# Cosines from squared half-angle sines in a filter generator, with its products and six tiles' statistics in other places

## The chip, the cores and the metric

The kernel runs on one core of one Trainium2 chip. The metric is the device time of one execution in microseconds (us), as the median of the runs shown; less is better. A core has engines that each work through an instruction queue of their own, in order: PE (TensorE, matmuls), DVE (VectorE), ACT (ScalarE), POOL (GpSimd) and SP, which here only issues DMAs. They wait for each other by semaphores.

## The reference, cut to what matters

Four layers on a 2048 x 640 activation: a long convolution (A), an attention (B), and both again with the same weights. Every layer is added to its input and starts with a layer norm.

```
def _A_ref(u, A_re, A_im, B_re, B_im, C_re, C_im, log_dt, Dskip):
    dt = jnp.exp(log_dt)[:, None]
    A, Bc, Cc = A_re + 1j * A_im, B_re + 1j * B_im, C_re + 1j * C_im
    P = jnp.exp((dt * A)[:, :, None] * l[None, None, :])      # l = 0 .. 2047
    K = jnp.einsum("dn,dnl,dn->dl", Cc, P, dt * Bc).real      # 640 channels, 128 states
    ...                                                       # y = u convolved with K
    return y + u * Dskip[None, None, :]
x = x + _A_ref(_layernorm(x), ...)
x = x + _B_ref(_layernorm(x), ...)
x = x + _A_ref(_layernorm(x), ...)
x = x + _B_ref(_layernorm(x), ...)
```

The change lies in the making of K, the filter of both convolutions: for every channel, state and time a complex exponential, that is a real exponential times a cosine and a sine, summed over the 128 states.

## The kernel before, in words

The program first makes the filter (`_kgen`), then its five spectra together with the first convolution (`kernel_spectra` and what follows), then attention, convolution and attention. In the profile `_kgen` ends at about 281 us of 2950.

**Generation.** Time is split as l = 32 i + s, so that an exponential of l is a product of one of i (64 values, tables with a 1) and one of s (32 values, tables with a 2). The states lie on the 128 partitions. The 640 channels go through in 20 units of 32, u = 0 to 19; each tile below is 128 x 1024 fp32, or near it. For each unit:

- PE makes phases into PSUM (`phase_first`, L424, tile `ph`, one buffer) in two halves h = 0 and 1, and exponents (`sizes`, L467, tile `pe`, two buffers) in three pieces k = 0, 1, 2, from bf16 tables `ta`, `tb`, `tm`.
- DVE turns a phase into an integer (`turns`, L433, tile `z`, one buffer) and shifts its whole turns out (`fraction`, L438, tile `f`, four buffers).
- ACT takes from each `f` the absolute value (L456, tile `fa`, one buffer), the sine (L457) and, from `fa` with a tile `halfpi` as bias, the cosine (L459). That is `trig`, twice a unit. From each `pe` it takes an exponential (`exps`, L475 and L477). Sines and exponentials are in different function tables, and an ACT_TABLE_LOAD stands at each change. To halve these, two units make a pair: exponentials of an even and the following odd unit stand together, and sines of the odd and the next even one.
- DVE multiplies exponentials with cosines and sines in six products (`products`, L485 to L494).
- PE sums over the states (`sums`, L504, tile `pk`), ACT copies the sums (`store`, L513), and after four units SP writes them to DRAM (`kd`). POOL clears the first columns of two tables a unit (L448, L449).

These steps are staggered by hand: in pass u of the loop ACT works on unit u, DVE on the phases of u + 1 and on the products of u - 1, PE on the sums of u - 2. `manual_schedule` keeps PE, ACT and DVE in the order in which the code is written. SP's and POOL's queues are ordered by a scheduler.

**What lies around it.** Ahead of the loop, `kg_tables` makes the tables on DVE and ACT and sends them through DRAM by DMA (SP queue). The first phase needs `tb`, the first exponent `tm` (L280). The activation x is loaded by eight DMAs of 640 KB (`load_x`, L685); tiles 0 to 3 of its 16 need the first two of these, tiles 4 to 7 the next two. Layer-norm statistics of a tile (`stats`: two L693, one L695) are DVE work: tiles 0 to 5 after the products of the last unit (u = 20), 6 to 9 in pass 21, and 10 to 15 among the butterflies of the first spectrum. Once PE has read the last table, `conv_weights` loads 4 MB of transform weights `wf` (L614). POOL loads the first channels of the filter back as `Rk` (L799), and PE starts the first spectrum (`raw`, L637, tile `zk`; ACT evicts it as `Ak`, L639; DVE adds and subtracts, L650 and on).

Of the kernel before, what the change touches and what calls it, by code (L numbers as in the profile page):

```python
# [202 lines left out]
class Net:  # L203
# [8 lines left out]
    def setup(self, ctx):  # L212
# [4 lines left out]
        self.halfpi = self.cp.tile([P, 1], F32, name="halfpi")  # L217
        nc.vector.memset(self.halfpi, 0.5 * math.pi)
# [144 lines left out]
    def _kgen(self, ctx):  # L363
# [39 lines left out]
        C1, S1, C2, S2, M1, M2, E1R, F, FA, Z, PH, PE_, PK, KST = ({} for _ in range(14))  # L403
# [23 lines left out]
        def turns(u, h):  # L427

            if (u, h) not in PH:
                phase_first(u, h)  # L430
            pp = PH.pop((u, h))
            Z[u, h] = bp.tile([P, 1024], I32, tag="z", bufs=1, name=f"z{u}{h}")
            nc.vector.tensor_scalar(Z[u, h], pp, 2.0**23, None, ALU.mult)  # L433

        def fraction(u, h):

            f = bp.tile([P, 1024], I32, tag="f", bufs=4, name=f"f{u}{h}")
            nc.vector.tensor_scalar(f, Z.pop((u, h)), 9, 9, ALU.logical_shift_left, ALU.arith_shift_right)  # L438
            F[u, h] = f

        def phase(u, h):
            turns(u, h)
            fraction(u, h)

        def trig(u, h):
            if h == 0:
                C1[u], S1[u] = big("c1", u, 33), big("s1", u, 33)
                nc.gpsimd.memset(C1[u][:, :, :, 0:1], 1.0)  # L448
                nc.gpsimd.memset(S1[u][:, :, :, 0:1], 0.0)  # L449
                s, c = swap(S1[u])[:, :, :, 1:33], swap(C1[u])[:, :, :, 1:33]  # L450
            else:
                C2[u], S2[u] = big("c2", u, 32, 3), big("s2", u, 32, 3)
                s, c = swap(S2[u]), swap(C2[u])
            f = F.pop((u, h))
            fa = bp.tile([P, 1024], F32, tag="fa", bufs=1, name=f"fa{u}{h}")
            nc.scalar.activation(fa, f, AF.Abs)  # L456
            nc.scalar.activation(s, f.rearrange("p (a d s) -> p a d s", a=2, d=16), AF.Sin,  # L457
                                 scale=TWO_PI / 2.0**23)
            nc.scalar.activation(c, fa.rearrange("p (a d s) -> p a d s", a=2, d=16), AF.Sin,  # L459
                                 scale=-TWO_PI / 2.0**23, bias=self.halfpi)  # L460
# [18 lines left out]
        def products(u, k):  # L479

            tt = nc.vector.tensor_tensor
            if k == 0:
                E1R[u] = big("e1r", u, 64, 2)
                er, m1, c1 = (fl(a[u]) for a in (E1R, M1, C1))
                tt(er[:, :, 32:64], m1[:, :, 32:64], c1[:, :, 0:32], ALU.mult)  # L485
                tt(er[:, :, 0:32], m1[:, :, 0:32], c1[:, :, 32:0:-1], ALU.mult)
            elif k == 1:
                m1, s1 = (fl(a.pop(u)) for a in (dict(M1), S1))
                nc.vector.scalar_tensor_tensor(m1[:, :, 32:64], m1[:, :, 32:64], -1.0, s1[:, :, 0:32],
                                               op0=ALU.mult, op1=ALU.mult)  # L490
                tt(m1[:, :, 0:32], m1[:, :, 0:32], s1[:, :, 32:0:-1], ALU.mult)
            else:
                tt(C2[u], C2[u], M2[u], ALU.mult)
                tt(S2[u], S2[u], M2[u], ALU.mult)  # L494
# [12 lines left out]
        def store(u):  # L507
# [5 lines left out]
            nc.scalar.activation(kst[:, :, 8 * g : 8 * g + 8], PK[u].rearrange("p (d i) -> p i d", d=8), AF.Copy)  # L513
# [15 lines left out]
        with tc.manual_schedule(engines=engines):  # L529
            for h in range(2):  # L530
                phase(0, h)
            for u in range(n + 3):
                now, nxt, prod, tot = u < n, u + 1 < n, 0 < u <= n, 2 <= u < n + 2
                odd = u % 2 == 1
                if u >= 3:
                    store(u - 3)
                if now and not odd:
                    trig(u, 0)
                if prod:
                    products(u - 1, 0)  # L540
                if now:
                    sizes(u, 0)
                    if odd:
                        exps(u, 0)
                if nxt:
                    phase_first(u + 1, 0)
                if now:
                    sizes(u, 1)
                    if odd:
                        exps(u, 1)  # L550
                if tot:
                    sums(u - 2, range(0, 1) if odd else range(0, 4))
# [1102 lines left out]
```

## Time and profile before

| What | us |
|---|---|
| median of 3 runs (2950.36 to 2952.25) | 2951.08 |
| the profiled execution: its time | 2951.75 |
| the profiled execution: its span, first to last instruction | 2950.0 |
| ahead of the loop (to the last `fraction` of unit 0) | 0 to 47.7 |
| first pair's exponentials | 54.4 to 62.8 |
| generation in a steady rhythm (the loads of the exponential table, 8 pairs) | 76.55 to 257.85 |
| first matmul of a spectrum | 280.75 |

The profiled execution is 0.67 us over the median, and 1.75 us of its time lie outside the span. In a row of the profile, "x16" counts instructions, then come their busy time in us and the mean of one in ns, then the idle time of that engine just ahead of them with what ended it. In the timeline the columns are start, duration, engine, line, operation and tiles; a bracket holds the idle time ahead. An instruction may start before the one ahead of it on its engine has ended, so that the distance of two starts, its pitch, is what a row of instructions costs. L numbers are lines of the kernel before, unless "after" is said.

### The profile page before, as it was taken

How to read it: one execution, taken by the hardware profiler on the slowest of the kernel's cores; microseconds unless marked ns; L12 is line 12 of the kernel's file. 1: busy time of each engine (PE TensorE's matmuls, PEld its weight loads, DVE VectorE, ACT ScalarE, POOL GpSimd, SP SyncE). 2: the span in 40 equal slices, each digit the busy share in tenths (PEclk: the TensorE clock that was granted, in tenths of full speed). 3: DMA queues.
4: the chain of work that ended last, by engine and by line, in shares of the span. 5: the costliest groups of instructions: out<-in, count | busy, mean ns of one | idle time of the engine just before them, and what ended most of it. 6: DMA issues, size and time to landing. Idle time of an engine off the chain costs nothing. (4 is left out here: it accounts for less than half of the span.)

```text
span 2950.0 us, 71583 instructions
## 1 busy us (share of the span) xinstructions
PE 2683.3 (91%) x29916; PEld 1557.6 (53%) x29916; DVE 2353.5 (80%) x2820; ACT 2386.6 (81%) x2905; POOL 294.5 (10%) x514
## 2 busy tenths in 40 slices
PE   2566989898899999999999998998999999999999
PEld 0234978774344444444444687773444444444444
DVE  7999999934688888888888699726788888888885
ACT  5997333455899999999999634338999999999997
POOL 0000011100210101011110011001101111111101
PEclk9767999998999999999999999998999999999999
DMA  6124545532211111111111256231111111111211
GB/s 147 35 30 141 193 114 112 147 116 84 93 33 37 32 37 34 35 34 35 36 34 33 93 115 160 67 126 47 36 34 39 51 32 36 51 35 34 55 31 31
DMA packets 156101, 196.31 MB, mean 67 GB/s; under 512 B 66220, under 2 KB 123532, under 8 KB 152148
## 3 DMA queue, kind: packets, MB, share of 16 engines
q1 hardware_dynamic: 119704, 141.90, 16.3%
q0 software_dynamic: 33776, 48.08, 7.9%
q8 instruction: 239, 3.92, 0.6%
q10 hardware_dynamic: 2288, 1.64, 0.2%
q14 instruction: 94, 0.77, 0.1%
HBM read 111.47 MB, written 48.55 MB: 54 GB/s over the span
## 5 line engine op out<-in xcount | busy, mean ns | idle before, releaser
L1360 ACT ACTIVATE ring<-ring 128x1024 f32<-128x1024 f32 (+1 forms) x680 | 738.2, 1086 | 0.4 <-DVE ring L1351 0.3
L1335 ACT ACTIVATE pt<-scb 128x1024 f32<-128x1024 f32 x684 | 692.1, 1111 | 26.5 <-PE scb L1325 24.8
L1335 ACT ACTIVATE pt<-scd 128x1024 f32<-128x1024 f32 x684 | 699.6, 1135 | 14.5 <-PE scd L1325 12.7
L1351 DVE COPY ring<-scd 128x1024 f32<-128x1024 f32 x307 | 375.2, 1222 | 82.4 <-PE scd L1325 63.0
L1351 DVE COPY ring<-scb 128x1024 f32<-128x1024 f32 x307 | 374.7, 1220 | 80.0 <-PE scb L1325 63.1
L1325 PE MATMUL scb<-qpb,kt 62*128 62x512 f32 x2048 | 365.5, 445 | 29.5 <-DVE ring L1351 14.4
L1325 PE MATMUL scd<-qpd,kt 62*128 62x512 f32 x2048 | 364.2, 444 | 19.1 <-ACT pt L1335 6.7
L1391 PE MATMUL pob<-pt,vt 128*32 128x256 f32 x5472 | 368.0, 387 | 0.0
L1391 PE MATMUL pod<-pt,vt 128*32 128x256 f32 x5472 | 367.1, 386 | 0.0
L1325 PEld LDWEIGHTS scb<-qpb,kt 62*128 62x128 f32 x2048 | 169.7, 186 | 249.2 <-ACT pt L1335 135.6
L1325 PEld LDWEIGHTS scd<-qpd,kt 62*128 62x128 f32 x2048 | 169.2, 185 | 239.8 <-ACT pt L1335 144.7
L1377 DVE SCALAR_TENSOR_TENSOR zh<-zh,zm 128x1024 f32<-128x1024 f32 x198 | 239.6, 1210 | 0.0
L1391 PEld LDWEIGHTS pob<-pt,vt 128*32 128x32 f32 x5472 | 143.3, 109 | 168.2 <-issue 109.4
L1391 PEld LDWEIGHTS pod<-pt,vt 128*32 128x32 f32 x5472 | 143.3, 109 | 165.6 <-issue 106.8
L1391 PE MATMUL pob<-ring,vt 128*32 128x256 f32 x2456 | 164.8, 381 | 0.4 <-ACT ring L1360 0.4
L1391 PE MATMUL pod<-ring,vt 128*32 128x256 f32 x2456 | 163.9, 379 | 0.4 <-ACT ring L1360 0.4
L1423 POOL DMA_DIRECT2D dn<-on x62 | 43.7, 705 | 1189.0 <-DVE on L1422 1152.1
L1429 POOL DMA_DIRECT2D rc<-ivd x248 | 126.5, 516 | 112.4 <-DMA ivd<-dn 108.4
L1460 DVE TENSOR_TENSOR x<-pyd,x 128x320 f32<-128x320 f32 x147 | 71.7, 488 | 77.2 <-PE pyd L1473 77.2
L1460 DVE TENSOR_TENSOR x<-pyb,x 128x320 f32<-128x320 f32 x147 | 71.7, 488 | 75.9 <-PE pyb L1473 75.8
L1473 PE MATMUL pyb<-wo,ot 128*32 128x320 f32 x1176 | 106.7, 434 | 6.3 <-DVE on L1422 5.6
L1473 PE MATMUL pyd<-wo,ot 128*32 128x320 f32 x1176 | 106.7, 434 | 5.7 <-DVE on L1422 4.9
(391 smaller groups left out, 4081.3 us busy)
## 6 DMA issues: line engine op xcount, KB each, us to landing
Akh<-kh SPq DMA_DIRECT2D x10, 2048.0 KB
rc<-ivd POOLq DMA_DIRECT2D x248, 64.0 KB, 2.2
kh<-Ak SPq DMA_DIRECT2D x5, 2048.0 KB
qhd<-qh SPq DMA_DIRECT2D x40, 256.0 KB
qld<-ql SPq DMA_DIRECT2D x40, 256.0 KB
qpb<-qhd SPq DMA_DIRECT2D x256, 40.0 KB
qpd<-qhd SPq DMA_DIRECT2D x256, 40.0 KB
ot<-on SPq DMA_DIRECT2D x216, 40.0 KB
```

The costliest lines, as they stand in the source:

```text
L1325: nc.tensor.matmul(sc[:, 512 * par : 512 * par + 512], kt[rows, 128 * t : 128 * t + 128], qps[nb, hg][rows, f].rearrange("p a c -> p (a c) ...
L1335: nc.scalar.activation(pt, sc, AF.Exp, scale=SCALE)
L1351: nc.vector.tensor_copy(cols, sc)
L1360: nc.scalar.activation(cols, cols, AF.Exp, scale=SCALE)
L1377: nc.vector.scalar_tensor_tensor(h, a, c[k], f, op0=ALU.add, op1=ALU.mult)
L1391: nc.tensor.matmul(po[32 * j : 32 * j + 32, 256 * f : 256 * f + 256], v[:, t], pt[j], start=(t == 0), stop=(t == 15))
L1423: nc.gpsimd.dma_start(den, on[20:128:32].rearrange("j (c r) -> j c r", c=32))
L1429: nc.gpsimd.dma_start(inv[32 * j : 32 * j + 32], self.ivd[hg % 2, j : j + 1].to_broadcast([32, 512]))
L1460: nc.vector.tensor_tensor(xh, py, xh, ALU.add)
L1473: nc.tensor.matmul(py[j : j + m], o[:, 128 * i + j : 128 * i + j + m], w[:, c0 : c0 + n], start=start, stop=stop)
```

## The change: what it does

Lines L430 to L620 of the kernel after hold it.

- **Cosines.** cos t = 1 - 2 sin(t/2)^2. `trig` now takes from `f` the sine of half the angle into the place of the cosine (after: L446) and the sine (L447). A new ACT instruction squares the first in place (`squares`, L454). The absolute value, the tiles `fa` and `halfpi` and the old cosine are gone. ACT has as many instructions as before.
- **Where the squares stand.** In odd passes each stands behind its two sines. In even passes they are put off (list `left`) and stand between the exponentials of that unit (`fill`).
- **Products.** The missing factor and the half are put into the products: five of six are now `scalar_tensor_tensor` with two constants, (c - 0.5) * m or (+-0.25 s) * m; `store` copies with a scale of 4.
- **Products behind phases.** `turns` writes `f` directly and `fraction` works in place (tile `z` is gone). Between a `turns` and its `fraction` there now stands a product.
- **Statistics.** Those of tiles 0 to 5 move from pass 20 to pass 0, ahead of the `turns` of unit 1; `load_x` stands earlier in the code, but SP's queue has its DMAs at the same places as before, and PE's instructions stand in the same order too.

On ACT, an even unit (4) and what follows it, before (c and s are cosine and sine tables, m exponentials; the number behind a name is the unit or a buffer):

```order
L475 ACT_TABLE_LOAD
L475 ACTIVATE m_4_732<-pe_637 128x16x64
L475 ACTIVATE m_4_732<-pe_643 128x16x64
L477 ACTIVATE m_4_733<-pe_735 128x2x16x32
L513 ACTIVATE kst_279<-pk_646 128x64x8
L475 ACTIVATE m_5_747<-pe_744 128x16x64
L475 ACTIVATE m_5_747<-pe_753 128x16x64
L477 ACTIVATE m_5_748<-pe_770 128x2x16x32
L456 ACTIVATE fa_780<-f_681 128x1024
L457 ACT_TABLE_LOAD
L457 ACTIVATE s_5_777<-f_681 128x2x16x32
```

The same place after:

```order
L469 ACT_TABLE_LOAD
L469 ACTIVATE m_4_730<-pe_639 128x16x64
L454 ACTIVATE c_4_630<-c_4_630 128x2x16x32
L469 ACTIVATE m_4_730<-pe_645 128x16x64
L454 ACTIVATE c_4_686<-c_4_686 128x2x16x32
L471 ACTIVATE m_4_731<-pe_734 128x2x16x32
L513 ACTIVATE kst_277<-pk_648 128x64x8
L469 ACTIVATE m_5_747<-pe_744 128x16x64
L469 ACTIVATE m_5_747<-pe_753 128x16x64
L471 ACTIVATE m_5_748<-pe_768 128x2x16x32
L446 ACT_TABLE_LOAD
L446 ACTIVATE c_5_775<-f_681 128x2x16x32
```

Two squares (L454) have come between the three exponentials of unit 4, and the absolute value ahead of the second table load has gone.

On DVE, the products of unit 5 with the phases of unit 7, before:

```order
L485 TENSOR_TENSOR e1r_872<-m_5_747,c_5_776 128x32x32
L486 TENSOR_TENSOR e1r_872<-m_5_747,c_5_776 128x32x32
L433 TENSOR_SCALAR z_917<-ph_878 128x1024
L438 TENSOR_SCALAR f_919<-z_917 128x1024
L489 SCALAR_TENSOR_TENSOR m_5_747<-m_5_747,s_5_777 128x32x32
L491 TENSOR_TENSOR m_5_747<-m_5_747,s_5_777 128x32x32
L433 TENSOR_SCALAR z_956<-ph_953 128x1024
L438 TENSOR_SCALAR f_958<-z_956 128x1024
L493 TENSOR_TENSOR c_5_849<-c_5_849,m_5_748 128x1024
L494 TENSOR_TENSOR s_5_850<-s_5_850,m_5_748 128x1024
```

And after:

```order
L490 SCALAR_TENSOR_TENSOR e1r_866<-c_5_775,m_5_747 128x32x32 x2
L431 TENSOR_SCALAR f_911<-ph_872 128x1024
L492 SCALAR_TENSOR_TENSOR m_5_747<-s_5_776,m_5_747 128x32x32
L436 TENSOR_SCALAR f_911<-f_911 128x1024
L492 SCALAR_TENSOR_TENSOR m_5_747<-s_5_776,m_5_747 128x32x32
L431 TENSOR_SCALAR f_947<-ph_944 128x1024
L490 SCALAR_TENSOR_TENSOR c_5_846<-c_5_846,m_5_748 128x1024
L436 TENSOR_SCALAR f_947<-f_947 128x1024
L494 TENSOR_TENSOR s_5_847<-s_5_847,m_5_748 128x1024
```

Each `fraction` (after: L436) has moved one product behind its `turns` (L431).

On DVE in the opening, after, with the semaphores that each instruction waits for:

```order
L436 TENSOR_SCALAR f_289<-f_289 128x1024 [waits DVE_49]
L723 BN_STATS st_316<-x 128x6 [waits DMAHW1_49,DMAHW0_49]
L723 BN_STATS st_316<-x 128x6
L725 BN_AGGR mv_65<-st_316 128x2 [waits DVE_49]
L723 BN_STATS st_320<-x 128x6 x2
L725 BN_AGGR mv_65<-st_320 128x2 [waits DVE_49]
L723 BN_STATS st_324<-x 128x6 x2
L725 BN_AGGR mv_65<-st_324 128x2 [waits DVE_49]
L723 BN_STATS st_328<-x 128x6 x2
L725 BN_AGGR mv_66<-st_328 128x2 [waits DVE_49]
L723 BN_STATS st_332<-x 128x6 [waits DMAHW3_49,DMAHW2_49]
```

Between the last `fraction` of unit 0 and the first `turns` of unit 1, which stood next to each other, there are now six tiles' statistics (the fifth begins in the last row, and the `turns` follows the sixth); the first waits for two DMA queues, the fifth tile (st_332) for two others.

The diff's core:

```diff
         def turns(u, h):
...
-            Z[u, h] = bp.tile([P, 1024], I32, tag="z", bufs=1, name=f"z{u}{h}")
-            nc.vector.tensor_scalar(Z[u, h], pp, 2.0**23, None, ALU.mult)
+            f = F[u, h] = bp.tile([P, 1024], I32, tag="f", bufs=4, name=f"f{u}{h}")
+            nc.vector.tensor_scalar(f, pp, 2.0**23, None, ALU.mult)
         def fraction(u, h):
-            f = bp.tile([P, 1024], I32, tag="f", bufs=4, name=f"f{u}{h}")
-            nc.vector.tensor_scalar(f, Z.pop((u, h)), 9, 9, ALU.logical_shift_left, ALU.arith_shift_right)
-            F[u, h] = f
+            f = F[u, h]
+            nc.vector.tensor_scalar(f, f, 9, 9, ALU.logical_shift_left, ALU.arith_shift_right)
         def trig(u, h):
...
-            fa = bp.tile([P, 1024], F32, tag="fa", bufs=1, name=f"fa{u}{h}")
-            nc.scalar.activation(fa, f, AF.Abs)
-            nc.scalar.activation(s, f.rearrange("p (a d s) -> p a d s", a=2, d=16), AF.Sin,
+            nc.scalar.activation(halves(u, h), f, AF.Sin, scale=0.5 * TWO_PI / 2.0**23)
+            nc.scalar.activation(swap(S2[u]) if h else swap(S1[u])[:, :, :, 1:33], f, AF.Sin,
                                  scale=TWO_PI / 2.0**23)
-            nc.scalar.activation(c, fa.rearrange("p (a d s) -> p a d s", a=2, d=16), AF.Sin,
-                                 scale=-TWO_PI / 2.0**23, bias=self.halfpi)
+        def halves(u, h):
+            return swap(C2[u]) if h else swap(C1[u])[:, :, :, 1:33]
+        def squares(u, h):
+            nc.scalar.activation(halves(u, h), halves(u, h), AF.Square)
...
+                if k == 0 or (k, part) == (2, 0):
+                    nc.vector.scalar_tensor_tensor(out, a, 0.5, b, op0=ALU.subtract, op1=ALU.mult)
+                elif k == 1:
+                    nc.vector.scalar_tensor_tensor(out, a, (-0.25, 0.25)[part], b, op0=ALU.mult, op1=ALU.mult)
+                else:
+                    nc.vector.tensor_tensor(out, a, b, ALU.mult)
...
+            left = []
+            def fill():
+                if left:
+                    squares(*left.pop(0))
             for u in range(n + 3):
...
                 if now and not odd:
                     trig(u, 0)
+                    left.append((u, 0))
...
+                if u == 0:
+                    for t in range(6):
+                        self.stats(t)
                 if nxt:
-                    phase(u + 1, 0)
+                    turns(u + 1, 0)
...
                 if prod:
-                    products(u - 1, 1)
-                if now:
-                    trig(u, 0 if odd else 1)
+                    products(u - 1, 1, (0,))
+                if nxt:
+                    fraction(u + 1, 0)
+                if prod:
+                    products(u - 1, 1, (1,))
+                if now and odd:
+                    trig(u, 0)
+                    squares(u, 0)
+                elif now:
+                    trig(u, 1)
+                    left.append((u, 1))
...
-                    else:
-                        exps(u, 0)
-                        sizes(u, 2)
-                        exps(u, 1)
-                        exps(u, 2)
...
-                for t in {n: range(6), n + 1: range(6, 10)}.get(u, ()):
-                    self.stats(t)
+                elif now:
+                    exps(u, 0)
+                    fill()
+                    sizes(u, 2)
+                    exps(u, 1)
+                    fill()
+                    exps(u, 2)
+                if u == n + 1:
+                    for t in range(6, 10):
+                        self.stats(t)
```

More of the change, by code (lines that the diff above doesn't have):

```diff
@@ L402, in _kgen @@
         units += [(2, r, 512 + 16 * r, 64, 64) for r in range(4)]
-        C1, S1, C2, S2, M1, M2, E1R, F, FA, Z, PH, PE_, PK, KST = ({} for _ in range(14))
+        C1, S1, C2, S2, M1, M2, E1R, F, PH, PE_, PK, KST = ({} for _ in range(12))
         KST[0, 0] = bp.tile([P, 64, 32], F32, tag="kst", bufs=2, name="kst00")
@@ L512, in store @@
             kst = KST[q, h]
-            nc.scalar.activation(kst[:, :, 8 * g : 8 * g + 8], PK[u].rearrange("p (d i) -> p i d", d=8), AF.Copy)
+            nc.scalar.activation(kst[:, :, 8 * g : 8 * g + 8], PK[u].rearrange("p (d i) -> p i d", d=8), AF.Copy,
+                                 scale=4.0)
             if g == 3:
@@ L530, in _kgen @@
             for h in range(2):
-                phase(0, h)
+                turns(0, h)
+                fraction(0, h)
+            left = []
+            def fill():
+                if left:
+                    squares(*left.pop(0))
             for u in range(n + 3):
@@ L534, in _kgen @@
                 odd = u % 2 == 1
+                if u == 0:
+                    self.load_x()
+                    nc.sync.dma_start(self.ident, ins["c_id"])
                 if u >= 3:
@@ L564, in _kgen @@
                 if nxt:
-                    phase(u + 1, 1)
+                    turns(u + 1, 1)
                 if prod:
-                    products(u - 1, 2)
+                    products(u - 1, 2, (0,))
+                if nxt:
+                    fraction(u + 1, 1)
+                if prod:
+                    products(u - 1, 2, (1,))
                 if tot:
                     sums(u - 2, range(5, 8) if odd else range(7, 8))
-                if now:
-                    if odd:
-                        trig(u, 1)
-                    else:
-                        exps(u, 0)
-                        sizes(u, 2)
-                        exps(u, 1)
-                        exps(u, 2)
-                if u == 0:
-                    self.load_x()
-                    nc.sync.dma_start(self.ident, ins["c_id"])
-                for t in {n: range(6), n + 1: range(6, 10)}.get(u, ()):
-                    self.stats(t)
+                if now and odd:
+                    trig(u, 1)
+                    squares(u, 1)
+                elif now:
+                    exps(u, 0)
+                    fill()
+                    sizes(u, 2)
+                    exps(u, 1)
+                    fill()
+                    exps(u, 2)
+                if u == n + 1:
+                    for t in range(6, 10):
+                        self.stats(t)
                 if u == n:
```

42 lines of the change are left out of this document (19 added, 23 removed).

## The prediction

> **What bounds the kernel now.** I looked first at the page of the profile, then at the busy times by stretch, since the change touches only the generation of the filter, which ends near 281 us. Columns of the second view: stretch, its length, then busy time (and instructions) of PE, weight loads, DVE, ACT, POOL, then granted clock and DMA.
>
> ```profile
> span 2950.0 us, 71583 instructions
> ...
> 76.55:257.85 181.30, 110.85 (x2208) 58.51 (x2208) 169.85 (x162) 172.72 (x176) 7.12 (x34) 0.69 0.18 29
> 280.75:297.10 16.35, 15.82 (x144) 15.74 (x141) 15.80 (x44) 4.69 (x5) 0.00 (x0) 1.00 0.84 221
> ```
>
> The first stretch is eight pairs of units, 181.30 / 8 = 22.66 us each. ACT is busy in 172.72 us of it, DVE in 169.85. Two engines so near to full need the timeline of a pair. This is ACT's, from one load of the exponential table to the next:
>
> ```profile
> 76.55 1.28 ACT L475 ACT_TABLE_LOAD   x1
> 77.84 1.94 ACT L475 ACTIVATE m<-pe 128x1024 f32<-128x1024 f32 x2
> 79.96 1.02 ACT L477 ACTIVATE m<-pe 128x1024 f32<-128x1024 f32 x1 [0.18 <-PE pe L467]
> 80.88 0.59 ACT L513 ACTIVATE kst<-pk 128x512 f32<-128x512 f32 x1
> 81.36 1.03 ACT L475 ACTIVATE m<-pe 128x1024 f32<-128x1024 f32 x1
> 82.63 1.02 ACT L475 ACTIVATE m<-pe 128x1024 f32<-128x1024 f32 x1 [0.24 <-PE pe L467]
> 84.18 1.02 ACT L477 ACTIVATE m<-pe 128x1024 f32<-128x1024 f32 x1 [0.53 <-PE pe L467]
> 85.10 1.05 ACT L456 ACTIVATE fa<-f 128x1024 f32<-128x1024 int32 x1
> 86.17 1.28 ACT L457 ACT_TABLE_LOAD   x1
> ...
> 88.44 1.15 ACT L459 ACTIVATE c<-fa,halfpi 128x1024 f32<-128x1024 f32 x1
> 89.62 1.06 ACT L456 ACTIVATE fa<-f 128x1024 f32<-128x1024 int32 x1
> 90.59 1.04 ACT L457 ACTIVATE s<-f 128x1024 f32<-128x1024 int32 x1
> 91.53 1.14 ACT L459 ACTIVATE c<-fa,halfpi 128x1024 f32<-128x1024 f32 x1
> 92.58 0.57 ACT L513 ACTIVATE kst<-pk 128x512 f32<-128x512 f32 x1
> ...
> 99.21 1.28 ACT L475 ACT_TABLE_LOAD   x1
> ```
>
> ACT never waits for DVE here. It waits three times for PE, 0.18 + 0.24 + 0.53 = 0.95 us. Each wait also loses the overlap of two instructions, 0.10, since neighbours start 0.92 apart (79.96 to 80.88) though one lasts 1.02. So 1.26 us of the 22.66 are lost to waits, and 21.40 are work. DVE does wait for ACT:
>
> ```profile
> L485 DVE TENSOR_TENSOR e1r<-m,c 128x1024 f32<-128x1024 f32 x16 | 19.5, 1221 | 6.5 <-issue 6.5
> L489 DVE SCALAR_TENSOR_TENSOR m<-m,s 128x1024 f32<-128x1024 f32 x16 | 19.5, 1218 | 0.0
> ...
> 82.65 1.22 DVE L433 TENSOR_SCALAR z<-ph 128x1024 int32<-128x1024 f32 x1
> 83.90 0.69 DVE L438 TENSOR_SCALAR f<-z 128x1024 int32<-128x1024 int32 x1
> 84.51 1.22 DVE L489 SCALAR_TENSOR_TENSOR m<-m,s 128x1024 f32<-128x1024 f32 x1
> 85.65 1.22 DVE L491 TENSOR_TENSOR m<-m,s 128x1024 f32<-128x1024 f32 x1
> ```
>
> The 6.5 us idle ahead of the first product (x16, one a unit) have no releaser in the view; the product reads exponentials and cosines, so I put them down to ACT. A unit on DVE is six products at a pitch of 1.14 (84.51 to 85.65), two turns at 1.25 and two fractions at 0.61: 6.84 + 3.72 = 10.56, a pair 21.1. So ACT sets the pace at 22.66, DVE has 1.5 us to spare.
>
> **ACT in a pair.** Out go four absolute values, three at 0.97 (89.62 to 90.59) and one at 1.07 ahead of the table load, and four cosines. A cosine costs 1.05 ahead of a copy (91.53 to 92.58) and 1.18 ahead of an absolute value (88.44 to 89.62), which rewrites the `fa` that the cosine reads. Two are of this kind, one stands ahead of a copy, and one ahead of a load, where it lasts its 1.14. That is 3.98 + 4.55 = 8.53. In come four sines of half angles and four squares. A half sine is the old sine with another constant, 0.94 to 0.97. No row shows a square of this size: it is bounded by the exponential's 0.92 below and the cosine's 1.18 above. I take 0.95, for like the absolute value and the sine it has no bias tile, and the tile it reads was written two instructions earlier, which cost the old cosine nothing (its `fa` too was two earlier). Eight at 0.95 are 7.60; the last exponential and the last sine now stand ahead of table loads and lose their overlap, 0.22. In: 7.82. **Work saved: 0.7 a pair.**
>
> The Trainium skill ("ScalarE: Activation LUTs", What ACT_TABLE_LOAD costs) says that an ACTIVATE takes the same time for every function, that a pointer operand adds about 93 ns, and that neighbours overlap by about 93 ns; an estimate from it for the square is 186 + 0.833 x 1024 - 93 = 946 ns. By it the sum below stays; by the cosine's row it would lose 8.3 us.
>
> Then the waits. PE refills two `pe` buffers behind ACT. With squares between the even unit's exponentials, the third piece is ready when ACT comes (0.28 gone), and so is the odd unit's second (0.34 gone): PE has the time of two squares more. The last wait is a path through PE:
>
> ```profile
> 81.54 1.06 PE L467 MATMUL pe<-kg,tm 48*128 48x512 bf16 x2
> ```
>
> From this start to the odd unit's last exponential (84.18) go 2.64 us. After the change this matmul can start when the even unit's third exponential has freed its buffer: 1.29 (load) + 0.92 + 0.95 + 0.92 + 0.95 + 1.02 = 6.05 into the pair. So the last exponential starts at 8.7; ACT would come at 1.29 + 3 x 0.92 + 2 x 0.95 + 0.48 + 2 x 0.92 = 8.27. It waits 0.4 instead of 0.63. **Waits saved: 0.8 a pair** (none at worst, 1.26 at best). Pair: 22.66 - 0.7 - 0.8 = 21.15; eight pairs 12.1.
>
> **DVE in a pair.** The products have the same size; `scalar_tensor_tensor` costs what `tensor_tensor` does (1218 and 1221). With a product between, a fraction no longer waits for its turns: 1.25 becomes 1.14, a unit 8 x 1.14 + 2 x 0.61 = 10.34, a pair 20.7. That is under ACT's 21.15, so it earns nothing by itself but keeps DVE from becoming the bound. The first product of an even unit needs the second exponential, which one square pushes back by 0.95; the hidden side of that is DVE's slack, 22.66 - 21.1 before, and now 21.15 - 20.7 = 0.45. DVE then runs a little later behind ACT, and ACT does not wait for it: the fraction that starts at 83.90 is the one that ACT takes up behind the copy of 92.58, 8 us on. POOL's clearing of columns follows the products of the unit two before.
>
> Against the interleaving speaks the Trainium skill ("VectorE: DVE Perf Modes", The DRAIN you can't avoid): the next operation starts only when the pipe is empty, and a semaphore between chained operations costs nothing more. By that rule a pair stays at 21.1 on DVE, still just under 21.15, and no saved wait beyond the forecast's would count. The pitch of 1.25 behind a dependent turns against 1.14 between products does not agree with it here.
>
> **Opening and tail.** Between the first pair's exponentials and the load at 76.55 stand four absolute values and four cosines (8.5); then there will be four half sines and two squares (5.9 with lost overlaps), for the other two squares come behind the load: **2.6 saved.** At the end these two have to be paid:
>
> ```profile
> 270.44 1.23 DVE L485 TENSOR_TENSOR e1r<-m,c 128x1024 f32<-128x1024 f32 x1 [2.37 <-ACT c L459]
> ```
>
> DVE's last six products wait for the last unit's cosine. On the way there from the last exponential load: two squares more (1.9), waits less (0.3), the last exponential's overlap (0.1), and half sine and square against absolute value and cosine (2.0 against 2.2): **1.5 lost.**
>
> **The statistics.** Where they go DVE waits for PE, and PE for a table's DMA; what they need was issued long before, and what they cost stands at their old place, where the seventh tile starts 6.01 us after the first:
>
> ```profile
> 4.04 2.72 SPq L685 DMA_DIRECT2D x<-in_A_u  x4
> 20.00 0.36 SPq L277 DMA_DIRECT2D hdth<-hth  x1
> 25.24 1.29 SPq L280 DMA_DIRECT2D tb<-hdth  x3
> 47.07 0.69 DVE L438 TENSOR_SCALAR f<-z 128x1024 int32<-128x1024 int32 x1
> 53.14 1.01 PE L467 MATMUL pe<-kg,tm 48*128 48x512 bf16 x2 [7.37 <-DMA tm<-hdare]
> 55.04 1.23 DVE L433 TENSOR_SCALAR z<-ph 128x1024 int32<-128x1024 f32 x1 [7.28 <-PE ph L424]
> 277.26 0.88 DVE L693 BATCH_NORM_STATS2 st<-x 128x6 f32<-128x320 f32 x2
> 283.27 0.83 DVE L693 BATCH_NORM_STATS2 st<-x 128x6 f32<-128x320 f32 x2
> ```
>
> They run from 47.76 to 53.8, the turns behind them is due at 55.04: hidden, with 1.3 to spare. The `tb` DMAs of 25.24 read what a DMA issued at 20.00, behind the four x loads on the same queue, had written, so I take x to have landed by then. At the old place they free nothing:
>
> ```profile
> 296.05 1.02 ACT L639 ACTIVATE Ak<-zk 128x1024 f32<-128x1024 f32 x1 [2.55 <-PE zk L637]
> 297.19 0.64 DVE L650 TENSOR_TENSOR B<-Ak 128x512 f32<-128x512 f32 x1
> ```
>
> DVE's last piece starts 0.12 after PE and ACT have delivered it (297.07), and PE is full from 280.75 on (15.82 of 16.35). **0 to 0.1.**
>
> **Sum.** 12.1 + 2.6 - 1.5 = 13.2 us by which the first spectrum starts earlier; all behind it keeps its order and moves along. The profiled execution's 2951.75 becomes 2938.6. It is 0.67 over the median, so on the median: 2951.08 - 13.2 = 2937.9.
>
> **Rivals.**
>
> *A wait for x (slower).* If the six tiles had to wait for all eight x loads, of which the last is issued at 78.37,
>
> ```profile
> 78.37 0.59 SPq L685 DMA_DIRECT2D x<-in_A_u  x1
> ```
>
> DVE would stand until 79 at least, statistics to 85, and the next turns 30 us late: 2951 + 30 - 13 = 2968. From a landing at 47.8 + 1.3 + 13.2 = 62.3 on the change loses. For it: x is one tile. Against it: the first and the fifth tile wait for two queues each, as separate loads would have it. Chance 0.05.
>
> *DVE becomes the bound.* A phase already comes late to DVE in some pairs:
>
> ```profile
> 109.67 1.22 DVE L433 TENSOR_SCALAR z<-ph 128x1024 int32<-128x1024 f32 x1 [0.66 <-PE ph L424]
> ```
>
> PE makes it behind the exponents, which now wait for ACT longer: if the wait grows to 1.0 in every pair and DVE cannot use it up as lag, a pair is 20.7 + 1.0 = 21.7 and the sum 7.7 + 1.1 = 8.8: 2942.3. For it: only 0.45 of slack. Against: the wait shrinks as DVE falls behind. Chance 0.15.
>
> *A square as dear as a cosine.* 36 squares at 0.23 more take 8.3 away: 4.9 are left, 2946.2; with all waits kept too, 2953. Chance 0.06.
>
> *The gain doesn't arrive.* The first spectrum needs `Rk` and weights by DMA:
>
> ```profile
> Rk<-kd POOLq DMA_DIRECT2D x1, 1024.0 KB, 8.6
> 264.66 0.69 POOL L799 DMA_DIRECT2D Rk<-kd  x1
> ```
>
> It landed at 273.3, 7.5 ahead of use, and its issue follows the same stores and moves with them. If something here stood still the time stays 2951. Chance 0.04.
>
> **How the numbers follow.** The forecast has the remaining 0.70. Its ends: no wait left gives 0.7 + 1.26 a pair, 15.7 + 2.6 - 1.1 = 17.2, 2933.9; all waits kept gives 0.7 a pair, 5.6 + 2.6 - 1.8 = 6.4, 2944.7. The range, 2934 to 2945, holds these and the second rival. A change of 0.2%, 5.9 us, is about what a measurement of this kernel can tell from none. Faster by more: forecast and second rival, 0.85. Within: third rival and the fourth, 0.10. Slower: 0.05, the first.
>
> **What would show it.** Loads of the exponential table 21.15 apart on ACT, the first near 74, the tenth near 243; a square at 1.04, no table load beside it; one wait of 0.3 to 0.4 for `pe` in a pair; fractions 1.14 behind what stands ahead; the first statistics at 47.8 with no wait for x; the first product of unit 19 near 257 and the first spectrum's matmul near 267.5. The prediction is wrong if ACT waits for DVE in the pairs, or if the spectrum starts early and the end does not move by as much.

## The result, and the profile after it

The changed kernel took 2934.24 us (median of 4 runs, 2931.56 to 2935.08) against 2950.72 for the kernel before on the same chip (2949.54 to 2952.25): a ratio of 0.9942, interval 0.9925 to 0.9960. It is 16.5 us faster; 13.2 were forecast. Four repetitions and near copies of it below (e1, e3, e10, e11) came out 18.8 to 20.2 us faster. The profiled execution took 2934.5. L numbers of the changed kernel are its own.

The page's first line, and the busy times by stretch of the same two stretches as before (length, then PE, weight loads, DVE, ACT, POOL, granted clock, DMA):

```profile
span 2932.7 us, 71549 instructions
...
74.40:244.01 169.61, 114.13 (x2220) 59.56 (x2210) 166.41 (x163) 166.47 (x176) 6.78 (x34) 0.70 0.16 31
268.48:284.83 16.35, 15.96 (x141) 15.87 (x142) 10.75 (x27) 4.69 (x5) 0.00 (x0) 1.00 0.77 221
```

Eight pairs now take 169.61 us, 21.20 a pair, where they took 22.66. The first spectrum starts at 268.48, 12.27 sooner than at 280.75, but the span is 17.3 shorter: some 5 us come from behind the generation. First one pair on ACT, in the timeline, with the load that ends it (the sines between are left out):

```profile
74.40 1.28 ACT L469 ACT_TABLE_LOAD   x1
75.70 1.02 ACT L469 ACTIVATE m<-pe 128x1024 f32<-128x1024 f32 x1
76.62 1.07 ACT L454 ACTIVATE c<-c 128x1024 f32<-128x1024 f32 x1
77.59 1.01 ACT L469 ACTIVATE m<-pe 128x1024 f32<-128x1024 f32 x1
78.49 1.06 ACT L454 ACTIVATE c<-c 128x1024 f32<-128x1024 f32 x1
79.44 1.02 ACT L471 ACTIVATE m<-pe 128x1024 f32<-128x1024 f32 x1
80.34 0.61 ACT L513 ACTIVATE kst<-pk 128x512 f32<-128x512 f32 x1
80.82 1.96 ACT L469 ACTIVATE m<-pe 128x1024 f32<-128x1024 f32 x2
83.11 1.03 ACT L471 ACTIVATE m<-pe 128x1024 f32<-128x1024 f32 x1 [0.33 <-PE pe L461]
84.15 1.28 ACT L446 ACT_TABLE_LOAD   x1
...
95.60 1.28 ACT L469 ACT_TABLE_LOAD   x1
```

A square stands between exponentials without a table load, at a pitch of 0.97 and 0.95 (76.62 to 77.59, 78.49 to 79.44). Two of the three waits for `pe` are gone, the third is 0.33. Now DVE, in the opening, in a pair, and at the last unit:

```profile
47.94 0.69 DVE L436 TENSOR_SCALAR f<-f 128x1024 int32<-128x1024 int32 x1
48.55 0.88 DVE L723 BATCH_NORM_STATS2 st<-x 128x6 f32<-128x320 f32 x2
...
54.43 0.21 DVE L725 BATCH_NORM_AGGREGATE mv<-st 128x2 f32<-128x12 f32 x1
55.56 1.23 DVE L431 TENSOR_SCALAR f<-ph 128x1024 int32<-128x1024 f32 x1 [0.92 <-PE ph L422]
...
82.58 1.23 DVE L431 TENSOR_SCALAR f<-ph 128x1024 int32<-128x1024 f32 x1
83.71 1.22 DVE L492 SCALAR_TENSOR_TENSOR m<-s,m 128x1024 f32<-128x1024 f32 x1
84.84 0.70 DVE L436 TENSOR_SCALAR f<-f 128x1024 int32<-128x1024 int32 x1
85.45 1.23 DVE L492 SCALAR_TENSOR_TENSOR m<-s,m 128x1024 f32<-128x1024 f32 x1
...
258.14 2.36 DVE L490 SCALAR_TENSOR_TENSOR e1r<-c,m 128x1024 f32<-128x1024 f32 x2 [2.64 <-ACT c L454]
```

The six tiles' statistics start right behind the fraction, wait for nothing, and leave 0.92 us of waiting for PE (0.42 in the repetition e1). Turns to product and product to fraction are 1.13 each. The steady idle ahead of the first product is gone; it is left at the end, for the last unit's square.

Behind the generation the order of the instructions is that of before, but transfers are faster. Medians from issue to landing of the copies that add onto a convolution's tile, from the view of DMA issues, before:

```profile
Aa<-Ra POOLq DMA_DIRECT2D x8, 512.0 KB, 7.3
Aa<-Akh POOLq DMA_DIRECT2D x8, 512.0 KB, 11.6
Ac<-Rc POOLq DMA_DIRECT2D x8, 512.0 KB, 7.3
Ac<-Akh POOLq DMA_DIRECT2D x8, 512.0 KB, 11.9
```

and after:

```profile
Aa<-Ra POOLq DMA_DIRECT2D x8, 512.0 KB, 6.2
Aa<-Akh POOLq DMA_DIRECT2D x8, 512.0 KB, 10.1
Ac<-Rc POOLq DMA_DIRECT2D x8, 512.0 KB, 6.3
Ac<-Akh POOLq DMA_DIRECT2D x8, 512.0 KB, 10.3
```

The same bytes, 1.0 to 1.6 us sooner. Waits shorten with them on two engines. One is ACT's for the load of the weights `wq`, in its timeline (last column), before and, in the next fence, after:

```profile
533.52 1.53 ACT L1072 ACTIVATE wh<-xnas 128x640 fp32r<-128x640 f32 x2 [12.71 <-DMA xnas<-in_B_wq]
```

```profile
518.59 1.52 ACT L1102 ACTIVATE wh<-xnas 128x640 fp32r<-128x640 f32 x2 [10.31 <-DMA xnas<-in_B_wq]
```

The other is DVE's in the second convolution, in the view of waits over 1640 to 1885 us (total, times, longest), before; after, both rows are missing:

```profile
DVE B L650 <- issue: 4.2, 2, 2.5
DVE B L650 <- DMA Ac<-Akh: 0.6, 1, 0.6
```

The first of these rows names no releaser ("issue": nothing that the profile shows). That it belongs to the copies is inferred from the runs below, where it goes and comes with them. Not all of this arrives. After the change a wait of the same adds for ACT has grown from 0.5 to 2.0 us, and one of 1.3 for DVE's own results is new. So I measure what is left by stretches: ACT's first `qh` of either attention, and its first eviction of the second convolution (`Ac`), before and, in the next fence, after.

```profile
594.65 0.59 ACT L1203 ACTIVATE qh<-pqb 52x512 fp32r<-52x512 f32 x1 [0.23 <-PE pqb L1191]
...
1665.45 1.02 ACT L639 ACTIVATE Ac<-zc 128x1024 f32<-128x1024 f32 x1 [5.71 <-PE zc L637]
...
1891.21 0.59 ACT L1203 ACTIVATE qh<-pqd 52x512 fp32r<-52x512 f32 x1 [0.21 <-PE pqd L1191]
```

```profile
580.65 0.59 ACT L1233 ACTIVATE qh<-pqb 52x512 fp32r<-52x512 f32 x1 [0.25 <-PE pqb L1221]
...
1650.98 1.02 ACT L669 ACTIVATE Ac<-zc 128x1024 f32<-128x1024 f32 x1 [5.71 <-PE zc L667]
...
1875.11 0.59 ACT L1233 ACTIVATE qh<-pqd 52x512 fp32r<-52x512 f32 x1 [0.22 <-PE pqd L1221]
```

From the first spectrum to the first `qh` it was 313.90 us and is 312.17, from `Ac` to the second attention's `qh` 225.76 and is 224.13. Together these two stretches, with the convolutions in them, give 3.4 of the 5 us. All else behind the first spectrum, nearly all of it attention, takes 2129.6 and 2127.9.

### The profile page after: what moved, and what is told of

Its sections match the earlier page's. It is cut to its first block, busy times and chain, and to the rows that moved or that the text cites. A ratio compares the mean times of both kernels' runs of the same rounds, so it can differ in the third digit from the quotient of the medians.

```text
span 2932.7 us, 71549 instructions
## 1 busy us (share of the span) xinstructions
PE 2690.0 (92%) x29916; PEld 1561.1 (53%) x29916; DVE 2350.0 (80%) x2819; ACT 2378.7 (81%) x2905; POOL 293.9 (10%) x514
## 3 DMA queue, kind: packets, MB, share of 16 engines
HBM read 111.47 MB, written 48.55 MB: 55 GB/s over the span
```

## The experiments

All were timed in five rounds beside the kernel before (2952.55, 2951.61, 2951.42 and 2950.67 us in the four groups: e1 to e4, e5 to e8, e9 to e11, e12). "Zero" is where the tiles of the convolutions begin, in bytes above a multiple of 256, "spectrum" the start of its first matmul, "wq wait" ACT's wait for those weights, "Aa from Akh" the median of those copies, "rest" the time from the spectrum's start to the end of the span. These and "pair" come from one profiled execution of each kernel.

| Run | zero | pair | spectrum | wq wait | Aa from Akh | rest | median | ratio |
|---|---|---|---|---|---|---|---|---|
| kernel before | 32 | 22.66 | 280.75 | 12.71 | 11.6 | 2669.3 | 2950.72 | 1 |
| e9_before_again | 32 | 22.66 | 280.65 | 12.69 | 11.5 | 2668.3 | 2951.01 | 0.9998 |
| e6_before_on_256 | 0 | 22.67 | 280.82 | 10.94 | 10.0 | 2663.9 | 2948.29 | 0.9987 |
| changed kernel | 0 | 21.20 | 268.48 | 10.31 | 10.1 | 2664.2 | 2934.24 | 0.9942 |
| e1_again | 0 | 21.19 | 267.38 | 10.37 | 9.9 | 2663.2 | 2932.39 | 0.9935 |
| e3_stats_back | 0 | 21.20 | 267.83 | 10.48 | 10.1 | 2663.6 | 2933.17 | 0.9934 |
| e4_squares_together | 0 | 22.04 | 274.86 | 10.28 | 10.1 | 2664.0 | 2940.70 | 0.9963 |
| e2_pad12 | 0 | 21.20 | 280.11 | 10.24 | 9.9 | 2662.8 | 2947.09 | 0.9984 |
| e10_attention_on_256 | 0 | 21.22 | 267.89 | 10.41 | 10.1 | 2660.9 | 2931.49 | 0.9939 |
| e11_fraction_adjacent | 0 | 21.19 | 267.90 | 10.16 | 10.1 | 2663.0 | 2932.67 | 0.9937 |
| e5_halfpi_back | 32 | 21.22 | 268.12 | 12.47 | 11.5 | 2666.6 | 2936.47 | 0.9946 |
| e7_offset_64 | 64 | 21.20 | 268.02 | 12.83 | 11.5 | 2665.7 | 2937.95 | 0.9950 |
| e8_offset_128 | 128 | 21.20 | 269.67 | 13.64 | 11.5 | 2666.5 | 2934.99 | 0.9940 |
| e12_pad12_halfpi | 32 | 21.19 | 281.04 | 13.86 | 11.4 | 2665.6 | 2949.87 | 0.9998 |

**e1_again**, the changed kernel itself, once more.

> The changed kernel itself, timed again beside the kernel before. The forecast's terms give a gain of 13.2 us; the profile of the changed kernel shows the first spectrum's first matmul 12.3 us earlier and the end 17.3 us earlier. Theory one (the generation's 12.3 us are all that the change gives; what comes behind, 4 to 5 us, is how PE's granted-clock windows and transfers happen to fall at the new start): the gain scatters around 12 to 17 from run to run. Theory two (the change itself shortens something behind the generation): the gain is 16 to 17 again, with the same stretches shorter.

0.9935 (0.9922 to 0.9949); the spectrum started 13.4 us sooner than before's, the end 19.4. By the medians it is 20.2 us faster, more than either theory had. The extra behind the generation is no chance of one execution.

**e2_pad12** puts the start of the spectra back to where it was: twelve copies on ACT, in the last unit, whose result nothing reads.

```diff
+    if u == n - 1:
+        for _ in range(12):
+            pad = bp.tile([P, 1024], F32, tag="pad", bufs=1, name="pad")
+            nc.scalar.activation(pad, F[u, 0], AF.Copy)
```

> The changed kernel with twelve more copies of a 128x1024 tile on ACT ahead of the last unit's sines (about 12 us, their output is read by nobody), so that the first spectrum starts about when it does in the kernel before. Theory one (all behind the generation depends on its start alone): the time of the kernel before, within 1.5 us. Theory two (the change shortens something behind the generation): 4 us less than the kernel before.

The spectrum started 0.6 us ahead of before's, the end came 7.1 sooner; 0.9984 (0.9975 to 0.9993). The profiled execution is the fastest of eleven; by the medians it is 5.5 us. The extra doesn't hang on an earlier start.

**e3_stats_back** leaves the statistics of tiles 0 to 5 behind the last unit's products, as before.

```diff
-    if u == 0:
-        for t in range(6):
-            self.stats(t)
...
+    for t in {n: range(6), n + 1: range(6, 10)}.get(u, ()):
+        self.stats(t)
```

> The changed kernel with the statistics of tiles 0 to 5 back in pass 20. By the forecast they are hidden in the opening and free nothing where they stood, so the first spectrum starts at the same time within 0.1 us and the time is the same. Theory two, in the form that six tiles less on DVE in front of the first spectrum is what shortens the later stages: 4 us slower than the changed kernel.

0.9934 (0.9920 to 0.9947), as with them moved. Moving them is worth nothing, and the extra is not theirs.

**e4_squares_together** puts the even passes' squares behind their sines, so that none stands between exponentials.

```diff
-    left.append((u, 0))
+    squares(u, 0)
...
-    left.append((u, 1))
+    squares(u, 1)
```

> The changed kernel with each square right behind its two sines in even passes too, none between exponentials. By the forecast the work stays (20.7 us a pair on ACT) and the three waits for PE come back as before (1.26 with the lost overlaps): 22.0 a pair instead of 21.2, 0.8 x 8 = 6.4 us slower at the tenth load of the exponential table, and as much at the end. If ACT's waits were not what the interleaving saves, the pair stays at 21.2 and the time with it.

0.9963 (0.9949 to 0.9977). ACT's timeline, one pair and then the tenth load of the exponential table, eight pairs on:

```profile
75.67 1.28 ACT L469 ACT_TABLE_LOAD   x1
...
79.08 1.02 ACT L471 ACTIVATE m<-pe 128x1024 f32<-128x1024 f32 x1 [0.18 <-PE pe L461]
...
81.75 1.02 ACT L469 ACTIVATE m<-pe 128x1024 f32<-128x1024 f32 x1 [0.24 <-PE pe L461]
83.30 1.02 ACT L471 ACTIVATE m<-pe 128x1024 f32<-128x1024 f32 x1 [0.53 <-PE pe L461]
...
252.03 1.28 ACT L469 ACT_TABLE_LOAD   x1
```

The three waits of before are back to the hundredth, and a pair is (252.03 - 75.67) / 8 = 22.04. So the square in place of absolute value and cosine is worth 22.66 - 22.04 = 0.62 a pair, its place between the exponentials 22.04 - 21.20 = 0.84. The extra is there as well.

What all four share with the changed kernel and not with before is an address. `halfpi` has four bytes, but takes 32 of each partition, and pools lay tiles one behind the other: without it `x` begins at byte 17024 in place of 17056, and `Ak`, `Akh`, `Rk`, `Ra`, `Aa`, `Rc`, `Ac`, `B`, `xna` and `xnas`, which lie behind it, on multiples of 256 in place of 32 above one. (`x` itself does not: it moves from 160 to 128 above one.) That the extra comes of this is theory three in the texts that follow; theory two is that the change shortens what is behind by itself.

**e5_halfpi_back** puts the tile back, for nobody:

```diff
 self.ident = self.cp.tile([P, P], F32, name="ident")
+self.halfpi = self.cp.tile([P, 1], F32, name="halfpi")
+nc.vector.memset(self.halfpi, 0.5 * math.pi)
```

> The changed kernel with one thing of before put back: the four-byte tile halfpi and its memset, allocated behind ident, where nothing uses it now. It takes 32 bytes of a partition, and so x, Rk, Ak, B, Aa, Ra, Akh, xnas and kt stand 32 bytes later again, where they stood before: at 32 above a multiple of 256 instead of on one. Nothing else moves. Theory three (the five us that the change gained behind the generation come of DMAs that got faster because these tiles now begin on a multiple of 256 bytes): the gain of the generation stays, the first spectrum matmul near 267.5 to 268.5, and what comes behind is lost again: the end moves by 12 to 13 us against before, a ratio of 0.9955 to 0.996 in place of 0.9935. The wq transfer into xnas that ACT waits for near 520 lands 2.4 us later than in the changed kernel (a wait of 12.7 us in place of 10.3), and the accumulating copies onto Aa and B take 7.3 and 11.3 us again in place of 6.2 and 9.6. Theory two (the earlier start, or the shorter generation, shortens what is behind by itself): the ratio stays at 0.9935, with a wait of 10.3.

The wait in ACT's timeline, and then DVE's in the view of waits (1620 to 1885 us):

```profile
520.43 1.53 ACT L1104 ACTIVATE wh<-xnas 128x640 fp32r<-128x640 f32 x2 [12.47 <-DMA xnas<-in_B_wq]
```

```profile
DVE B L682 <- issue: 3.6, 2, 1.9
DVE B L682 <- DMA Ac<-Akh: 0.3, 1, 0.3
```

Both are back, and the copies take 7.3 and 11.5. The rest is 2666.6, 2.4 to 3.4 longer than in the changed kernel and its repetition; 0.9946 (0.9933 to 0.9960). The signs are as theory three has them, the size is smaller than its 5 us: a ratio of 0.9955 to 0.996 was expected. By the time alone this run can't be told from the changed kernel (0.9942, 0.9935 in e1).

**e6_before_on_256** aligns the kernel before: 224 bytes of filler behind `halfpi`.

```diff
+self.pad = self.cp.tile([P, 56], F32, name="pad")
+nc.gpsimd.memset(self.pad, 0.0)
```

> The kernel before, with a tile of 224 bytes a partition that nothing uses, behind halfpi: together 256 bytes, so that x, Rk, Ak, B, Aa, Ra, Akh, xnas and kt begin at the same places within 256 bytes as in the changed kernel. Nothing of the change is in it. Theory three: the generation keeps its time (the first spectrum matmul within 1 us of before's 280.75), and the end comes 4.5 to 6.5 us sooner, a ratio of 0.998; the wait of ACT for the wq transfer is 10.3 in place of 12.7. Theory two: no difference, a ratio of 1.000, and a wait of 12.7.

The same wait in ACT's timeline:

```profile
529.76 1.53 ACT L1074 ACTIVATE wh<-xnas 128x640 fp32r<-128x640 f32 x2 [10.94 <-DMA xnas<-in_B_wq]
```

The wait is 10.94 where 10.3 was expected. Copies of 6.4 and 10.0, the two rows of DVE's waits gone, the generation as before: 0.9987 (0.9978 to 0.9996), 3.3 us faster by a tile that nothing uses. The span of the profiled execution, one of the fastest of eleven, is 5.3 shorter. Here none of the change is in the kernel, so theory two falls as the account of these 3.3 us.

**e7_offset_64** and **e8_offset_128** are the changed kernel with a filler of 64 or 128 bytes behind `ident`.

> The changed kernel with a tile of 64 bytes a partition behind ident that nothing uses: the same tiles begin at 64 above a multiple of 256. It tells what the multiple is. If 64 bytes are what counts, all stays as in the changed kernel: a ratio of 0.9935, a wq wait of 10.3. If 256 bytes count, the gain behind the generation goes as with halfpi: a ratio of 0.9955 to 0.996, a wait near 12.7. By the Trainium skill (DMA: Bandwidth & Descriptors, How a descriptor splits into AXI transactions) the piece of a descriptor before the first multiple of 256 is fetched whole, which would make 64 a little dearer than 32; that sentence would give a wait above 12.7.

> The changed kernel with a tile of 128 bytes a partition behind ident that nothing uses: the tiles begin at 128 above a multiple of 256. If 64 or 128 bytes are what counts: as the changed kernel, a ratio of 0.9935. If 256 bytes count: a ratio of 0.9955 to 0.996 or above it. By the Trainium skill's account (DMA: Bandwidth & Descriptors, How a descriptor splits into AXI transactions) an access of 1024 bytes that begins at 128 fetches 1152 bytes in place of 1056 at 32, an estimate of 9 per cent more for each copy of such rows; then it would be slower than with halfpi back, by about 1 to 3 us.

Copies of 7.2 and 11.5 in both, as at 32. So of the offsets tried 0 alone is fast, which makes the multiple 256 (not 512: `Ra` begins at 76032, 297 x 256), and how far above it makes no difference to the copies. The waits for `wq`, 12.83 and 13.64, rise with the offset, as the last sentence expected for e7 has it, but at 32 they run from 12.47 to 13.86, so they decide nothing. The ratios, 0.9950 and 0.9940, both fall short of the expected 0.9955 to 0.996; they are inside each other's intervals, and 0.9940 is no slower than the changed kernel. What tells these runs from it are the copies and the rests, 2665.7 and 2666.5, which are with the others off the multiple.

**e9_before_again** is the kernel before.

> The kernel before itself, profiled and timed once more. Against its profile, all seven other profiles lie 1.3 to 3.5 us further ahead at the end than the starts of the generation and the copies onto the multiple of 256 bytes account for, wherever the tiles begin. If that rest is how one execution of the kernel before differs from another, this profile's span is 1 to 3 us shorter than 2950.0, with the same start of the spectrum (280.75 within 0.5) and the same wait for the wq transfer (12.7). If the rest belongs to the change, this profile agrees with the first to within 1 us at every stage, and the rest stays without a cause.

Its span was 1.1 shorter, from the same start and with the same waits. So a single execution wanders by about a microsecond, at the low end of the expected 1 to 3; that explains a part of what was to be explained.

**e10_attention_on_256** moves `qpb`, `qh`, `rq`, `on` and others of the attention's tiles from 64 above the multiple onto it; `ot`, `rc` and `mt` stay off it:

```diff
 off = ap.tile([P, 1], F32, name="off")
+gap = ap.tile([P, 48], F32, name="gap")
+nc.gpsimd.memset(gap, 0.0)
```

> The changed kernel with a tile of 192 bytes a partition that nothing uses ahead of obr in the attention: qpb, qh, rq, on, dn and wo begin on a multiple of 256 bytes instead of 64 above one, in both halves; ot, rc and mt move from 192 to 128 above one. If transfers end waits in the attention as they do in the convolution, this is faster still: the stretches 560 to 1640 and 1860 to 2930 hold nearly all of the span, with 512 transfers of q, and 0.5 per cent of it would be 10 us. My theory: no difference (a ratio of 0.993 to 0.995, the end within 2 us of the changed kernel's), since in the attention no engine but POOL waits long for a transfer (DVE 13.8 us in all, PE none): a faster transfer ends no wait there. By the rival, 0.990 to 0.992.

0.9939 (0.9925 to 0.9952), 2931.49 us: the lowest median of all, but no difference from the changed kernel that these runs can tell. The profiled execution ended 3.9 us before the changed kernel's, outside the 2 us expected, and 1.8 before e1's. A gain of some 2 us is not excluded, the rival's 10 us are.

**e11_fraction_adjacent** puts each fraction right behind its turns (shown for the first half, h = 0; the second has the same edit).

```diff
 turns(u + 1, 0)
+fraction(u + 1, 0)
 ...
-fraction(u + 1, 0)
 ...
```

> The changed kernel with each fraction right behind its turns on DVE, as the kernel before had them, the products behind both. Four such pairs stand in a pair of units. In the changed kernel DVE was busy 20.7 to 21.2 us of each 21.2. My forecast's price (1.25 in place of 1.13 us when the fraction follows what it reads): DVE's pair grows by 0.4 to 0.5 us, past ACT's, so that the table loads come 21.3 to 21.6 us apart in place of 21.20, and the end 1 to 3 us later than the changed kernel's, a ratio near 0.9945. By the Trainium skill (VectorE: DVE Perf Modes, The DRAIN you can't avoid), which has a wait between chained operations free, no difference: turns to fraction 1.13, loads 21.20 apart, a ratio of 0.9935.

DVE's timeline, two units apart in its first and last row, and ACT's second and tenth load of the exponential table:

```profile
124.59 1.22 DVE L431 TENSOR_SCALAR f<-ph 128x1024 int32<-128x1024 f32 x1
...
128.72 1.22 DVE L431 TENSOR_SCALAR f<-ph 128x1024 int32<-128x1024 f32 x1
129.97 0.69 DVE L436 TENSOR_SCALAR f<-f 128x1024 int32<-128x1024 int32 x1
...
145.66 1.22 DVE L431 TENSOR_SCALAR f<-ph 128x1024 int32<-128x1024 f32 x1
```

```profile
73.75 1.28 ACT L469 ACT_TABLE_LOAD   x1
...
243.29 1.28 ACT L469 ACT_TABLE_LOAD   x1
```

The price is there, 1.25 (128.72 to 129.97) in place of 1.13, and DVE's pair is 21.07. The expectation drawn from it was wrong: 21.07 is still under ACT's 21.2, the loads stay (243.29 - 73.75) / 8 = 21.19 apart, and the time is 0.9937 (0.9923 to 0.9950).

**e12_pad12_halfpi** has the edits of e2 and e5 together.

> The changed kernel with both additions: twelve copies of 128x1024 on ACT into a tile that nothing reads, ahead of the last unit's sines, and the unused tile halfpi, by which all tiles behind it begin 32 bytes above a multiple of 256 again. So the first spectrum starts where before's does (280 to 281), and the tiles lie where before's lie; what stays of the change are the generation's instructions. In the profiles so far, the time from the first spectrum matmul to the end of the span was 2660.9 to 2664.2 us in eight kernels whose tiles begin on the multiple, and 2665.7 to 2669.3 in five whose tiles don't. Theory three: 2665.7 to 2669.3 here, a wq wait of 12.4 to 12.9, copies of 7.3 and 11.5 us, a ratio of 0.999 to 1.000 (with the twelve copies alone it was 0.9984). If the 2 us that before and its repetition lie above the changed kernels off the multiple come of the start alone, 2668 to 2669.3; if they come of the change itself or of chance, 2665.7 to 2667. Theory two (the change shortens what is behind by itself): 2661 to 2664.

0.9998 (0.9989 to 1.0007), against 0.9984 with the padding alone: the copies 7.3 and 11.4 again, the rest 2665.6, a hair under the stated 2665.7. The wait for `wq`, 13.86, missed the stated 12.4 to 12.9. Theory two had 2661 to 2664. The start alone makes no 2 us.

## Why the prediction was right, and where it failed

*ACT in a pair: right.* 21.20 for 21.15. Square and half sine for cosine and absolute value gave 0.62 (forecast 0.7), the waits 0.84 (0.8); one wait of 0.33 plus its lost overlap stays, where 0.4 was forecast. Eight pairs gave 181.30 - 169.61 = 11.69 of 12.1. The square's pitch of 0.95 to 0.97 is the forecast's value; the cosine's 1.18 is out. An estimate from the figures of the Trainium skill ("ScalarE: Activation LUTs", What ACT_TABLE_LOAD costs) was 946 ns; the trace agrees.

*Opening and tail: right.* The tenth load came at 244.01 (243 forecast), the second at 74.40 for 76.55: 2.15 of 2.6. I put the rest down to transfers of the opening that landed later in this execution: the first exponent matmul, which waits for `tm`, started at 53.66, in the repetition at 52.83. Of nine other kernels with the same pairs eight have that matmul at 52.83 to 53.23 and the second load at 73.56 to 73.95, that is 2.6 to 3.0 saved; e12 has 53.70 and 74.43. From the tenth load to the spectrum went 24.47 us in place of 22.90: 1.57 lost, 1.5 forecast.

*Statistics and DVE: right.* No wait for x at 48.55, 0.92 to spare (1.3 forecast; 0.42 in e1); e3 shows that nothing hangs on it. DVE's pair without its waits is 2 x (8 x 1.13 + 2 x 0.61) = 20.5 (20.7 forecast). DVE did not become the bound: ACT waits for nothing but PE in all eight pairs, and by e11 DVE can take on half a microsecond more. The rule of the Trainium skill that a wait between chained operations is free ("VectorE: DVE Perf Modes", The DRAIN you can't avoid) doesn't agree with e11's 1.25 against 1.13, if the wait is what makes the difference; no run puts a fraction that waits for nothing behind a turns. A chain on 128x12 tiles in the changed kernel (from 297.80 on) points the same way: starts lie 0.20 to 0.21 apart where each operation reads the one ahead of it, 0.09 to 0.11 where it doesn't. What the forecast made of it, that it earns nothing, holds.

*Gain of the generation: right.* 11.69 + 2.15 - 1.57 = 12.27 in this profile, 12.6 to 13.4 in e1, e3, e5, e7, e10 and e11, 13.2 forecast. In e8 it is 11.1, with a wait of 1.63 for the filter's load.

*The filter's load: a wrong reason.* "Its issue follows the same stores and moves with them" is not so. The timeline of POOL and PE after:

```profile
260.24 0.58 POOL L829 DMA_DIRECT2D Rk<-kd  x1 [9.64 <-ACT s L447]
...
268.48 1.60 PE L667 MATMUL zk<-Rk,wf 128*128 128x128 f32 x12
```

POOL now waits with `Rk` for ACT's last sine. Before, `z` and a tile `f` of even units lay where `Rk` will; without `z` the tiles `f` have moved down, and the one of unit 19's second half lies there too. So the load waits for the last reader of `f`. Of the 7.5 us that it landed ahead of use nothing is left: it was issued at 260.24 and took 8.2 to land, which gives 268.4; in e1 and e11 the first spectrum waits 0.25 and 0.29 us for it, in e8 1.63. The rival that the gain doesn't arrive was nearer than its 0.04 said.

*The step that failed: "all behind it keeps its order and moves along".* The order did stay, but what is behind became 5.0 us shorter (2669.3 to 2664.2); the sum had no term for it. The change removed a tile, which the prediction mentioned only as the cosine's bias. With it the tiles of both convolutions moved onto multiples of 256 bytes, the copies onto them took 13 to 15 per cent less time, and waits on DVE and ACT shrank: theory three. The rests fall into two groups that don't touch: 2660.9 to 2664.2 in eight profiles on the multiple, 2665.6 to 2669.3 in six off it. Like with like, the effect is 4.9 us in the kernel before (2668.8, the mean of two, to 2663.9) and 3.0 in the changed one (means of 2666.1 and 2663.1). By the medians it is less sure: 3.3 in the kernel before, 2.3 in the changed one (a mean ratio of 0.9945 in e5, e7 and e8 against 0.9937 in e1, e3, e10, e11 and the changed kernel).

The two stretches with the convolutions show it most clearly. Together they are 538.6 to 540.6 us in the six profiles off the multiple and 534.5 to 536.6 in the eight on it. All else behind the first spectrum takes 2126.5 to 2129.6 off it and 2125.1 to 2129.3 on it: no difference, and a scatter of 4 us of its own.

The 17.3 us of this profile are thus 12.3 of generation, 3.4 in the two stretches with the convolutions, which is the size of the alignment's effect, and 1.7 in the rest, inside its scatter. The median, 2934.24, comes out at the low end of the range, 2934, but that end stood for something else: a generation with no wait left, 17.2 us earlier. The generation gave 12.3. So the nearness to that end is luck, and the repetition e1, 20.2 us faster than the kernel before beside it, lies beyond it. The sign that was named, a spectrum that starts early and an end that does not move by as much, came the other way round: the end moved by more.

What stays open: off the multiple, the two profiles of before have rests 2.7 us longer, in the mean, than the four of the changed kernel. About 1.2 of that lies in the two stretches with the convolutions, the rest in the attentions, whose scatter is larger; e12 rules out the start. That the `wq` load lands later because it shares the DMA engines with the slower copies, and not by its own rows in `xnas`, was argued and not tried apart.

## What to carry to other kernels

A tile that is removed or added moves everything that is allocated behind it: compare the addresses of the two builds as well as their order, and ask which transfers read or write what moved. Put the tiles that many large DMAs copy between on multiples of 256 bytes. A filler cost no time here, but it paid only where an engine waits for the transfer (3 us or more in the convolutions; in the attention nothing that the runs can tell). Between two engines near their limits, filling one's waits with its own work was worth more than the cheaper operation (0.84 against 0.62 a pair).

## What the runs showed of the hardware

A DMA that adds rows of 1024 bytes from `Ra` onto `Aa`, 512 KB in all, took 6.2 to 6.4 us where both begin on a multiple of 256 bytes, and 7.2 to 7.3 where they begin 32, 64 or 128 above one; those issued behind it, from `Akh`, 9.9 to 10.1 against 11.4 to 11.6. Between `Rc` and `Ac`, in the second convolution, it was 6.3 to 6.9 and 7.3 to 7.4. In all these copies both ends moved together, so no run tells whether the reading or the writing end counts.

The Trainium skill ("DMA: Bandwidth & Descriptors", How a descriptor splits into AXI transactions) has each transaction start on a multiple of 256; where a descriptor does not, the bytes ahead of its start are fetched unused and still cost beats of 32 bytes. The multiple agrees. By an estimate from that page, with a row as one descriptor, such a row takes five transactions in place of four, and 33 beats at 32 and 36 at 128, in place of 32. That the loss grows with the offset does not agree: 7.3, 7.2 and 7.2 us at 32, 64 and 128.

One kind of copy kept its time and has no explanation here: `Ra` onto `B`, two copies, took 6.1 in both kernels, while `Rc` onto `B` went from 7.1 to 6.4.
